# Attention and MLP in one kernel: from emission by budget to a hand-ordered pipeline of 32 head-pair steps

## Chip, core, metric

One core of a Trainium2 chip. The metric is device time in microseconds. Every time of a kernel is a median of several executions. Comparisons use runs in the fast state: a run counts as slow when it is over 1.5% above the fastest of the same kernel in its call. The kernel before itself spreads over 3%, so that in the call of e8, e9 and e11 seven of its eleven runs count as slow and in that of e12 six; the recorded medians of before in these calls include them, the ratios do not.

## The reference, cut to what matters

```python
# 8 batches, 8 heads, 576 queries, 16 beacon keys ahead of 576 keys, D = 64
scores = (q @ k_all.T) / sqrt(64); scores = where(causal, -1e9, scores)
a = exp(scores - max); a /= a.sum(-1)
x = (a @ v_all)                      # heads side by side: 4608 tokens x 512
h = x @ w_in                         # 512 -> 2048
out = (h * sigmoid(1.702 * h)) @ w_out   # 2048 -> 512
```

Beacon keys are seen by every query; the others are causal. Both kernels work in fp16 with fp32 sums, without subtracting the maximum, and use tanh for the sigmoid.

## The kernel before

It keeps scores transposed (keys on partitions) so that exp(scores) is at once an operand of AV. A pair of heads uses rows 0 to 63 and 64 to 127 of TensorE. The parts that the argument touches:

```python
# mask: a matmul of identity x tmask (-30000) into the scores' PSUM
nc.tensor.matmul(scA[0:kkw, 0:mw], ident[:, 0:kkw], tmask[:, mc0:mc0+mw], start=False, stop=True)
nc.scalar.activation(out=EjA[...], in_=scA[...], func=AFT.Exp, scale=0.125)   # one head, <= 512 columns
# AV: lhs = V and one column of ones, 65 columns; row 64 of the result is Z
nc.scalar.copy(out=zcb[r0:r0+1, 0:512], in_=oA[64:65, :])
# every four heads: 1/Z, then broadcast by a matmul with ones, then multiply on VectorE
nc.vector.reciprocal(out=rz[0:97, :], in_=zcb[0:97, :])           # 97 x 576
nc.tensor.matmul(pbc[0:64, :], ones128[r0:r0+1, :], rz[r0:r0+1, 0:512], ...)
nc.vector.tensor_tensor(out=xT[p][...], in0=pbc[0:64, :], in1=ox[...], op=ALU.mult)
# MLP1 tile: 4 matmuls of 384 columns, tanh on ScalarE, gate on VectorE (frees PSUM)
nc.scalar.activation(out=sig, in_=hps, func=AFT.Tanh, scale=0.851)
nc.vector.scalar_tensor_tensor(out=gt[...], in0=sig, scalar=1.0, in1=hps, op0=ALU.add, op1=ALU.mult)
# after each pair: up to 16 units of MLP in a row; where there is none, three warm-up matmuls
pump_mlp(MLP_BUDGET)
```

All PSUM comes from one pool of eight banks.

The softmax here doesn't subtract the row's maximum and nothing guards it: scores larger than these inputs give would overflow.

## Time and profile before

| | before |
|---|---|
| median of three runs | 540.97 us (535.39 to 541.63) |
| span of the profiled run | 536.4 us |
| mean granted TensorE clock | 0.916 |
| first MLP matmul | 68.6 us |
| two batches in the steady part (from one 64-matmul piece of the chain at 112.84 to the same piece at 239.00) | 126.16 us, so 63.1 a batch |

Part 1 of the page (busy time and share of each engine), the groups of three lines by form (line, engine, operation, shapes, count; busy us and mean ns; idle before), and the row of windows for the two batches (length, busy us of PE, PEld, DVE, ACT and POOL, clock, DMA share, GB/s), all of the kernel before:

```profile
PE 489.2 (91%) x3204; PEld 257.6 (48%) x3204; DVE 298.8 (56%) x553; ACT 271.5 (51%) x741; POOL 120.9 (23%) x164
```

```profile
L254 DVE RECIPROCAL rz<-zcb_cur 97x576 f16<-97x576 f32 x16 | 60.0, 3753 | 6.2 <-ACT zcb_cur L248 6.2
...
L187 PE MATMUL pu<-tmask,ident 128*128 128x128 f16 x96 | 23.2, 241 | 0.0
...
L201 ACT ACTIVATE EjA<-pu 128x512 f16<-128x512 f32 x32 | 19.1, 595 | 64.3 <-PE pu L194 39.0 <-PE pu L187 25.1
```

```profile
112.84:239.00 126.16, 120.62 (x800) 63.91 (x800) 74.34 (x139) 67.23 (x185) 27.33 (x35) 0.91 0.50 48
```

The shares alone say "TensorE, 91%". Three things qualify that. Busy time of a matmul is longer than the room it takes (an MLP2 matmul counts 389 ns in the groups by form, while one follows another every 216 ns), so overlapping matmuls hide idle slots. The clock of 0.91 in the steady part makes the same work longer. And one line of VectorE, the reciprocal, takes 3.75 us, five to eight times as long as the engine's other large groups (456 to 680 ns); everything behind it waits, as in the trace, where VectorE starts nothing else between 130.02 and 133.69 us.

### The profile page before, as it was taken

To read this page: it belongs to the slowest core of one execution; us is meant where nothing else is said; L and a number is where in the kernel's file an instruction comes from. 1 tells how busy PE (TensorE), PEld (TensorE's weight loads), DVE (VectorE), ACT (ScalarE), POOL (GpSimd) and SP (SyncE) were. 2 spreads that over 40 slices of the span, in tenths; PEclk is the share of its full clock that TensorE was granted. 3 is DMA by queue.
4 is the path that set the end of the run, shared out by engine and by line. 5 is a ranking of instruction groups with operands and counts; after the bars stand their busy time and mean duration, and the time that the engine had idled before them with its cause. 6 is when DMAs were issued, how large, how long until landed. Compare 5 with 4: busy or idle time off the path is not lost.

```text
span 536.4 us, 8324 instructions
## 1 busy us (share of the span) xinstructions
PE 489.2 (91%) x3204; PEld 257.6 (48%) x3204; DVE 298.8 (56%) x553; ACT 271.5 (51%) x741; POOL 120.9 (23%) x164
## 2 busy tenths in 40 slices
PE   1996998999999999999999999989989999949997
PEld 0453554555435455555445445545544545525543
DVE  1236587497624367677842436977851625878400
ACT  0472667467714269358631448577641446627411
POOL 9568850540004500270000900060000000000000
PEclk9997798599789999689969999899969999869999
DMA  9999990990016910190002960090001010000022
GB/s 94 175 173 142 93 89 2 66 70 1 2 39 74 160 40 2 12 122 3 2 0 79 125 88 21 2 89 2 1 0 72 29 59 21 1 1 2 20 79 78
DMA packets 122919, 28.59 MB, mean 53 GB/s; under 512 B 115712, under 2 KB 117760, under 8 KB 122880
## 3 DMA queue, kind: packets, MB, share of 16 engines
q0 software_dynamic: 117696, 18.62, 46.9%
q1 hardware_dynamic: 5184, 9.44, 4.6%
q8 instruction: 25, 0.41, 0.3%
q14 instruction: 14, 0.11, 0.1%
HBM read 37.22 MB, written 9.44 MB: 87 GB/s over the span
## 4 chain that ended last, share of the span: by engine, by line
PE 67%; ACT 11%; DVE 7%; POOL 5%; issue 5%; DMA 4%; ACTq 0%; DVEq 0%; POOLq 0%
PE pu L326 24%; PE pu L302 18%; PE pu L229 5%; PE pu L170 4%; ACT EjA L201 3%; PE pu L147 3%; DVE rz L254 3%; DMA w<-in_moe_w_in_dram 3%; PE pu L135 3%; PE pu L187 3%; ACT zcb_cur L247 3%; ACT EjB L207 2%; ACT sig L313 2%; DVE ox L244 2%; DVE g L314 2%
## 5 line engine op out<-in xcount | busy, mean ns | idle before, releaser
L302 PE MATMUL pu<-xT,w 128*128 128x384 f16 x768 | 131.3, 331 | 1.8 <-DVE g L314 1.1
L326 PE MATMUL pu<-w,g 128*128 128x512 f16 x576 | 130.8, 389 | 0.0
L313 ACT ACTIVATE sig<-pu 128x384 f16<-128x384 f32 x192 | 91.7, 491 | 51.7 <-PE pu L302 33.4
L201 ACT ACTIVATE EjA<-pu 128x512 f16<-128x512 f32 (+2 forms) x192 | 83.8, 442 | 64.9 <-PE pu L194 39.0
L314 DVE SCALAR_TENSOR_TENSOR g<-sig,pu 128x384 f16<-128x384 f16 x192 | 100.7, 549 | 26.5 <-ACT sig L313 17.4
L302 PEld LDWEIGHTS <-w 128*128 128x128 f16 x768 | 75.1, 99 | 55.1 <-issue 7.8
L244 DVE CAST ox<-pu 64x512 f16<-64x512 f32 x64 | 43.2, 675 | 101.6 <-PE pu L229 55.5
L326 PEld LDWEIGHTS <-g 128*128 128x128 f16 x576 | 56.7, 100 | 71.4 <-issue 8.3
L103 POOL DMA_DIRECT2D qb<-in_q_dram x40 | 34.5, 879 | 222.9 <-PE pu L135 218.4
L207 ACT ACTIVATE EjB<-pu 128x512 f16<-128x512 f32 (+2 forms) x192 | 83.0, 448 | 0.5 <-PE pu L194 0.2
L334 ACT ACTIVATE osb<-pu 128x512 f32<-128x512 f32 x36 | 21.5, 597 | 112.9 <-PE pu L326 94.7
L254 DVE RECIPROCAL rz<-zcb_cur 97x576 f16<-97x576 f32 x16 | 60.0, 3753 | 6.2 <-ACT zcb_cur L248 6.2
L177 PE MATMUL pu<-qTp,kTp 64*128 64x512 f16 (+2 forms) x192 | 56.9, 312 | 2.2 <-DVE g L314 1.4
L170 PE MATMUL pu<-qTp,kTp 64*128 64x512 f16 (+2 forms) x192 | 55.8, 313 | 3.4 <-ACT EjA L201 1.9
L247 ACT COPY zcb_cur<-pu 1x512 f32<-1x512 f32 x64 | 36.9, 577 | 31.0 <-DVE ox L244 30.0
L140 DVE COPY qTp<-pu 128x576 f16<-128x576 f16 x32 | 14.6, 456 | 56.3 <-PE pu L135 56.2
L283 DVE TENSOR_TENSOR xT<-pu,ox 64x512 f16<-64x512 f32 x64 | 43.5, 680 | 2.2 <-PE pu L261 0.7
L229 PEld LDWEIGHTS <-vb 128*65 128x65 f16 (+1 forms) x320 | 36.6, 129 | 9.1 <-issue 4.9
L236 PEld LDWEIGHTS <-vb 128*65 128x65 f16 (+1 forms) x320 | 35.5, 129 | 6.9 <-issue 1.9
L187 PE MATMUL pu<-tmask,ident 128*128 128x128 f16 (+2 forms) x160 | 38.4, 240 | 0.0
L194 PE MATMUL pu<-tmask,ident 128*128 128x128 f16 (+2 forms) x160 | 37.5, 234 | 0.0
L261 PE MATMUL pu<-rz,ones 1*64 1x512 f16 x64 | 17.5, 462 | 20.2 <-ACT zcb_cur L247 12.4
(42 smaller groups left out, 436.7 us busy)
## 6 DMA issues: line engine op xcount, KB each, us to landing
out_dram<-osb SPq DMA_DIRECT2D x36, 256.0 KB, 2.0
qb<-in_q_dram POOLq DMA_DIRECT2D x32, 128.0 KB, 4.4
kb<-in_k_dram POOLq DMA_DIRECT2D x32, 128.0 KB, 4.9
vb<-in_v_dram POOLq DMA_DIRECT2D x24, 128.0 KB, 4.4
w<-in_moe_w_in_dram POOLq DMA_DIRECT2D x4, 512.0 KB, 10.5
w<-in_moe_w_out_dram POOLq DMA_DIRECT2D x16, 128.0 KB, 4.9
vb<-in_v_dram POOLq DMA_DIRECT2D x8, 112.0 KB, 3.6
vb<-in_v_dram POOLq DMA_DIRECT2D x8, 80.0 KB, 4.8
```

The source lines that it names most:

```text
L170: nc.tensor.matmul(scA[0:kkw, 0:w], kTp[0:64, kk0 : kk0 + kkw], qTp[0:64, s0 + c : s0 + c + w], start=True, stop=not do_mask,)
L177: nc.tensor.matmul(scB[0:kkw, 0:w], kTp[64:128, kk0 : kk0 + kkw], qTp[64:128, s0 + c : s0 + c + w], start=True, stop=not do_mask,)
L187: nc.tensor.matmul(scA[0:kkw, 0:mw], ident[:, 0:kkw], tmask[:, mc0 : mc0 + mw], start=False, stop=True,)
L201: nc.scalar.activation(out=EjA[0:kkw, c : c + w], in_=scA[0:kkw, 0:w], func=AFT.Exp, scale=0.125,)
L207: nc.scalar.activation(out=EjB[0:kkw, c : c + w], in_=scB[0:kkw, 0:w], func=AFT.Exp, scale=0.125,)
L229: nc.tensor.matmul(oA[0 : D + 1, s0:512], lhs, ej[0:kkw, 0:wA], start=(j == 0), stop=(j == NJ - 1),)
L244: nc.vector.tensor_copy(out=ox[0:64, 0:512], in_=oA[0:64, :])
L254: nc.vector.reciprocal(out=rz[0:97, :], in_=zcb[0:97, :])
L302: nc.tensor.matmul(hps[:, :], w1t[kp][:, nt * P : (nt + 1) * P], xT[kp][:, tok0 : tok0 + MB], start=(kp == 0), stop=(kp == NKP - 1),)
L313: nc.scalar.activation(out=sig[:, :], in_=hps[:, :], func=AFT.Tanh, scale=0.851)
L314: nc.vector.scalar_tensor_tensor(out=gt[:, MB * blk : MB * blk + MB], in0=sig[:, :], scalar=1.0, in1=hps[:, :], op0=ALU.add, op1=ALU.mult,)
L326: nc.tensor.matmul(ops[:, :], gts[(r, nt)][:, mt * P : (mt + 1) * P], w2t[nt][:, :], start=(nt == 0), stop=(nt == NNT - 1),)
```

## The change

The intent: one step for each of the 32 pairs of heads, in which four score chunks of pair i, four AV halves of pair i-1 and transposes for the next batch are emitted with eight MLP slots between them (a slot is one MLP1 tile of 512 columns or a quarter of an MLP2 tile). The core of the 852-line diff, with cuts:

```diff
-                nc.tensor.matmul(scA[0:kkw, 0:mw], ident[:, 0:kkw], tmask[...], start=False, stop=True)
-                nc.scalar.activation(out=EjA[...], in_=scA[0:kkw, 0:w], func=AFT.Exp, scale=0.125)
+        nc.scalar.activation(out=E[:, :, choff[ci]:choff[ci]+o], in_=sc[:, :, 0:o], func=AFT.Exp, scale=0.125)  # both heads
+            if i < 8:   # mask on exp's output: min with 0 / 65504
+                    nc.vector.tensor_tensor(out=E[...], in0=E[...], in1=keep[...], op=ALU.min)
+            else:
+                nc.gpsimd.affine_select(out=blk, in_=blk, compare_op=ALU.is_ge, fill=0.0, ...)
...
-        lhs = vb[0:kkw, j, h, 0 : D + 1]
+        lhs = vb[0:kw, j, h, :]          # V beside 64 columns of ones: Z comes out on 64 rows
-        nc.vector.reciprocal(out=rz[0:97, :], in_=zcb[0:97, :])
-                nc.tensor.matmul(pbc[0:64, :], ones128[...], rz[...], ...)
+    z_gather(b, hf)   # DMA: Z of four heads to 64 partitions x 36 columns
+    z_recip(b, hf)    # next step: reciprocal of 36 columns, DMA to DRAM, DMA back, broadcast
+    norm(b, hf)       # the step after: 4 multiplications on GpSimd into xT
...
+    pss = ...(bufs=2)  # scores, two banks each
+    psu = ...(bufs=3)  # MLP1, AV, transposes
+    pso = ...(bufs=1)  # MLP2
...
+    for i in range(NSTEP + LAG):
+        run_later(i)                       # z_recip, norm, "batch ready"
+        ... att = 4 score chunks, 4 AV halves, [z_gather], transposes
+            if p == 0:
+                load_qk(nb, 0, H); load_bk(nb)      # next batch, GpSimd's queue, behind norm
+        for a in range(n):
+            att[a]()
+            want = (a + 1) * QUOTA // n
+            while done < want: mlp_slot(); done += 1
```

The mask matmuls, the broadcast matmuls, the warm-up matmuls, the copies of Z and the long reciprocal go. GpSimd gets masks and normalisation on top of issuing all input loads.

## The prediction

> **What bounds the kernel now.** I read the page first (busy tenths, granted clock, DMA row), then the chain of work that ended last in order of time, then the timeline of one pair of heads, then the table of windows.
>
> ```profile
> PE   1996998999999999999999999989989999949997
> ...
> PEclk9997798599789999689969999899969999869999
> DMA  9999990990016910190002960090001010000022
> ```
>
> TensorE is busy almost throughout, but its clock is not whole: the mean granted clock is 0.916. One window shows what a dip is:
>
> ```profile
> 142.20:152.40 10.20, 9.54 (x46) 4.46 (x47) 5.35 (x13) 4.08 (x15) 0.00 (x0) 0.50 0.01 2
> 500.00:520.00 20.00, 20.00 (x97) 9.29 (x95) 2.22 (x4) 4.50 (x9) 0.00 (x0) 1.00 0.14 53
> ```
>
> The clock (third figure from the end) is 0.50 in the first and 1.00 in the second. If it is always one or the other, (1 - 0.916)/0.5 = 17% of 536.4 us, some 90 us, ran at half clock, which costs up to 45 us. The chain tells what surrounds those stretches:
>
> ```profile
> 16.80 14.82 DMA w<-in_moe_w_in_dram
> ...
> 68.56 10.54 PE pu L302 x64
> ...
> 130.02 3.75 DVE rz L254
> 133.77 0.88 DVE g L314 x2
> ...
> 172.82 13.83 PE pu L326 x64
> ```
>
> (Columns: start, length, what.) Three readings. The first 68.6 us have no MLP: inputs and weights come in, and the POOL queue stands behind the w1 transfers. A dense MLP matmul of 512 columns takes 13.83/64 = 216 ns, one of 384 takes 10.54/64 = 165 ns (162 in the clean parts). And in between, a 3.75 us reciprocal over 97 rows holds VectorE while TensorE waits for the g that frees its PSUM. The two MLP groups are 768 x 162 ns + 576 x 216 ns = 249 us; so 536 - 249 - 68 = 219 us go to attention, softmax denominators, half clock and waits after the start. That is what the change can win.
>
> **What the Trainium skill says.** "TensorE: Matmul & The Clock Gate", Part 1, has a clock of half or whole rate only, whole after a busy window of about 3.4 us, half after an idle one. The windows above agree (0.50 and 1.00). "TensorEngine Tiling (Array Packing)", Key Properties: changing the tiling mode drains the engine, and separate tiles run in parallel. The timeline agrees with both:
>
> ```profile
> 123.32 0.39 PE L170 MATMUL pu<-qTp,kTp 64*128 64x512 f16 x1
> 123.32 0.39 PE L177 MATMUL pu<-qTp,kTp 64*128 64x512 f16 x1
> 123.64 0.22 PE L187 MATMUL pu<-tmask,ident 128*128 128x112 f16 x1
> ```
>
> Both heads' score matmuls (64 rows each) start together, so the pair costs one; the 128-row mask matmul starts 0.32 us later rather than 0.216, so a switch costs about 0.1 us (0.095 over many such pairs). "DMA: Bandwidth & Descriptors", SWDGE vs HWDGE vs iDMA: a casting transfer must come from GpSimd; here all loads of inputs and weights do, at 879 to 916 ns of POOL time each (part 5 of the page). "GPSIMD Engine Reference", 3.1: a two-input elementwise op takes about 2.6 cycles per element at 1.2 GHz. The kernel before has no such op, so the normalisation below is an estimate from that page.
>
> **The change, part by part, on TensorE at whole clock.**
> MLP: 144 tiles x 4 x 216 = 124.4 us, and 36 x 16 x 216 = 124.4 us: 248.8 us, the same columns as before.
> Scores: for a pair of heads 512+64+336+80+464+208 = 1664 columns, both heads together, 0.71 us; four chunks with two mode switches each, 8 x 0.095 = 0.76 us. So 1.47 us a pair, 47 us for 32. The mask matmuls go (40 groups of 128 columns and some, about 67 ns each: 320 x 67 = 21 us, plus half of the switches that they forced).
> AV: 1664 columns for each of two heads in 18 matmuls, 1.45 us a pair, 46 us. Before it was about 1.5, so no gain there.
> Transposes: q and k of a pair are 10 matmuls. Before, four of 128 columns take 66 ns each and the 64-row one with its switch 132: 0.40 us for five. So 0.79 us a pair plus 0.44 us a batch for the beacon: about 26 us, and some 7 more for the first batch's 96-column form.
> The 1/Z broadcast (L261, L270: 128 matmuls, some 18 us), the 36 warm matmuls (8 us) and the reciprocal of 3.75 us x 16 go. Z now comes out of AV on 64 rows and takes a way through DRAM with reciprocals of 36 columns (about 0.3 us), three steps ahead of its use.
> Sum for TensorE: 249 + 47 + 46 + 33 = 375 us. It stays the bound.
>
> The others, by rows of before. ScalarE: exp of four chunks of 1024, 960, 928 and 416 columns; a 512-column activation takes 595 ns, back to back a stretch of N columns costs about 0.83N + 60 ns, so 3.0 us a step and 96 us in all (167 us busy before in twice-as-many small ones); tanh 144 x 0.6 = 86, output 36 x 0.6 = 21, q copies 32 x 0.67 = 21: about 225 to 240 us. VectorE: gate 144 x 0.68 = 98 (549 ns for 384 columns, plus 128/0.96), AV copies 128 x 0.44 = 56, k copies 15, masks of the first eight steps about 13: 190 us. POOL: 148 issues x 0.88 = 130, masks 120 x 0.4 = 48, normalisation 64 x 1.4 = 90: 268 us. All below TensorE.
>
> **The time, stage by stage.** The start. Step 0 can begin at about 6 us. But step 1 already transposes batch 1, whose q and k are issued behind w1 on the same queue. Before, by 50 us four tensors' worth had landed (batch 0, w1, w2, batch 1's q and k: 14.3 MB read, 300 GB/s); after, q and k of batch 1 come after batch 0 and w1, 10 MB, about 34 us; w2, V of batch 1 and q, k of batch 2 then come one after another until about 58 us, where step 5 wants them. So step 7, the first with MLP slots (batch 0 is marked ready there), begins at about 64 to 66 us. That is no earlier than before, with one more pair done.
> From there TensorE has 249 of MLP, 25 x 1.47 of scores, 26 x 1.45 of AV and 19 of transposes: 342 us.
> PSUM waits. MLP1, AV and transposes share three banks (before: eight for all). An MLP1 tile holds its bank for 0.65 + 0.39 (the last matmul's end) + 0.60 tanh + 0.68 gate = 2.35 us. With AV halves in between, the fourth claim comes after 2.1 us; the wait is some 0.28 us a slot, about 1.2 us in a step with eight MLP1 tiles; there are 14 of those: 17 us. MLP2 has one bank: 0.17 + 0.05 + 0.6 us until it is emptied, against 0.36 us of other work, so 0.45 us at most of 36: with the last ones about 12 us.
> Masks and normalisation on POOL behind eleven issues (10 us) in the first step of a batch: 1 us a batch, 8 us. Tail: output scaling 0.6 and store 2 us, 3.5 us.
> Sum: 66 + 342 + 17 + 12 + 8 + 3.5 = 448.5; measured medians lie some us above the profiled span (541 against 536): 451 us.
>
> **The rivals.** (a) Three PSUM banks are too few and ScalarE or VectorE become the pace. For: a step of eight MLP1 tiles has 3.0 + 4.8 us of ScalarE and 7.7 us of VectorE in some 11 us, each in strict order, so a tile's 2.35 us can grow to 3.3. Against: before, 64 MLP1 matmuls ran at 165 ns with the same chain of tanh and gate. Each further 0.5 us a tile costs 14 x 8 x 0.5 = 56 us at worst: 480 to 500. (b) POOL becomes the bound. For: 34 us of its work in a batch of about 47, in order, with issues ahead of masks that AV needs, and a two-input op on 64 partitions that no trace here prices. If it takes twice my estimate, POOL is at 45 of 47 us: 470 to 490. (c) Nothing waits: slots cover the waits, the start shortens because the first batch's q and k move in longer pieces and MLP starts at 55 us: 375 + 35 = 410 us. (d) The transfers eat the gain: the start stays on DMA until 80 us, as the issues of batch 1 wait behind w1: 465.
>
> **Range and chances.** Floor 375 plus an empty start is about 400; I see no way under 410. (a), (b) and (d) together would make 500. Eight in ten: 418 to 488. For a result within 2% of 541, some 80 us of new waits would have to arise beyond those counted: 3%; slower: 2%.
>
> **What would show each step.** Start: the first L302-like matmul at about 65 us, after a wait for a DMA of batch 1 or 2. Clock: mean at 0.94 or more and 1.00 after 70 us; if it dips there, the windows have idle stretches that I don't foresee. MLP matmuls at 216 ns of dense running. PSUM: TensorE's waits in the mlp1 lines put down to VectorE's gate at 0.2 to 0.5 us, some 20 us in all, and waits of MLP2 for ScalarE's scaling about 12 us. Rows: exp of 1024 columns near 1.04 us, normalisation near 1.4 us, POOL near half busy. Wrong would be: waits of AV for POOL masks over 15 us, of MLP1 for POOL's normalisation, or TensorE's own sum over 400 us at whole clock.

## The result

| | before | after |
|---|---|---|
| median | 538.18 us (4 runs) | 476.66 us (475.82 to 480.68, 4 runs) |
| profiled span | 536.4 us | 474.5 us |
| mean granted clock | 0.916 | 0.941 |
| first MLP matmul | 68.6 us | 89.8 us |
| from there to the end | 467.8 us | 384.7 us |
| a steady batch | 63.1 us | 48.2 us |

The ratio is 0.8879 (95% interval 0.8807 to 0.8951). A ratio is the mean time of one kernel's fast runs over that of the other's in the same rounds, so it is not quite the ratio of the medians quoted. The gain of 62 us has two parts of opposite sign: the part after the first MLP matmul became 83 us shorter, the start 21 us longer.

The kernel after, part 1 and rows of part 2 of its page (40 slices of 11.9 us):

```profile
PE 396.0 (83%) x2584; PEld 201.8 (43%) x2584; DVE 193.0 (41%) x410; ACT 222.8 (47%) x341; POOL 251.3 (53%) x348
...
PE   2505555889999999899989998999899999899985
...
PEclk9955675899999999999999999999999999999999
DMA  9999939959614981399129911990203112100111
```

Nearly all half-clock time is now in the first eight slices. (1 - 0.941)/0.5 x 474.5 is 56 us, as estimated for before, where it was 90 us all along the run. The row of windows for one steady batch and three groups of part 5:

```profile
190.64:238.84 48.20, 44.54 (x293) 21.91 (x292) 19.92 (x39) 25.95 (x41) 32.23 (x47) 1.00 0.80 85
```

```profile
L392 DVE SCALAR_TENSOR_TENSOR g<-sig,u 128x512 f16<-128x512 f16 x144 | 99.0, 687 | 104.9 <-ACT sig L391 104.8
L354 POOL TENSOR_TENSOR xT<-O,rz 64x576 f16<-64x576 f32 x64 | 89.6, 1400 | 79.9 <-DMA rz<-zd 76.3
...
L274 POOL TENSOR_SCALAR_AFFINE_SELECT E<-E 128x256 f16<-128x256 f16 (+2 forms) x120 | 43.1, 395 | 67.0 <-ACT E L252 66.3
```

The clock is 1.00 throughout the batch. VectorE has 20 us of work in 48, GpSimd 32. The view of waits (engine, line, what was waited for: us in total, times, longest), from the first MLP matmul to the end, has just these for TensorE:

```profile
PE u L382 <- DVE g L392: 12.4, 20, 0.7
PE o L408 <- ACT osb L417: 9.7, 25, 0.7
PE s L244 <- ACT E L252: 2.3, 5, 0.5
```

L382 is MLP1 and waits for the gate to free one of three banks; L408 is MLP2 and waits for its single bank; L244 is a score chunk and waits for exp. Together they come to 24.4 us, under 1 us each.

Where did the start go? The chain of work that ended last, of the kernel after, in order of time (start, length, what):

```profile
18.18 11.96 DMA w<-in_moe_w_in_dram
...
33.54 4.91 DMA bk<-in_beacon_k_dram
...
48.54 5.64 DMA zc<-O
...
57.16 4.40 DMA rz<-zd
61.70 1.40 POOL xT L354
...
67.83 4.25 POOL qn L114 x5
72.08 2.88 POOL kn L114 x4
...
76.20 3.43 DMA bk<-in_beacon_k_dram
```

Batch 1's beacon arrives at 38.4 us because its issue stood behind w1. Then Z of the first two pairs goes to DRAM and back, GpSimd normalises (61.7 to 67.5 us), and only behind that it issues batch 2's q, k and beacon, which arrive at 79.6 us. The transposes of batch 2 stand in TensorE's order before the first MLP slot.

So the first theory, "Q": GpSimd's strict order makes loads wait for Z. Its rival, "D": the DMA engines are full in the start, and the order is of no matter.

### The profile page after: what moved, and what is told of

It reads as the page before. It is cut to its first block, busy times and chain, and to the rows that moved or that the text cites. A ratio compares the mean times of both kernels' runs of the same rounds, so it can differ in the third digit from the quotient of the medians.

```text
span 474.5 us, 6853 instructions
## 1 busy us (share of the span) xinstructions
PE 396.0 (83%) x2584; PEld 201.8 (43%) x2584; DVE 193.0 (41%) x410; ACT 222.8 (47%) x341; POOL 251.3 (53%) x348
## 4 chain that ended last, share of the span: by engine, by line
PE 59%; ACT 17%; POOL 7%; DMA 7%; DVE 5%; issue 4%; ACTq 0%; POOLq 0%; DVEq 0%
PE o L408 26%; PE u L382 19%; ACT E L252 8%; PE u L310 6%; ACT sig L391 5%; PE u L189 4%; DVE g L392 4%; PE s L244 3%; ACT osb L417 3%; DMA w<-in_moe_w_in_dram 3%; DMA bk<-in_beacon_k_dram 2%; POOL kn L114 1%; POOL vb L136 1%; DMA zc<-O 1%; POOL xT L354 1%
## 5 line engine op out<-in xcount | busy, mean ns | idle before, releaser
L382 PE MATMUL u<-xT,w 128*128 128x512 f16 (+1 forms) x640 | 144.7, 358 | 12.5 <-DVE g L392 12.4
L408 PE MATMUL o<-w,g 128*128 128x512 f16 x576 | 144.1, 379 | 9.7 <-ACT osb L417 9.7
L392 DVE SCALAR_TENSOR_TENSOR g<-sig,u 128x512 f16<-128x512 f16 x144 | 99.0, 687 | 104.9 <-ACT sig L391 104.8
L354 POOL TENSOR_TENSOR xT<-O,rz 64x576 f16<-64x576 f32 x64 | 89.6, 1400 | 79.9 <-DMA rz<-zd 76.3
L391 ACT ACTIVATE sig<-u 128x512 f16<-128x512 f32 x144 | 87.6, 609 | 77.3 <-PE u L382 72.9
L252 ACT ACTIVATE E<-s 128x1024 f16<-128x1024 f32 (+3 forms) x128 | 104.7, 876 | 14.8 <-PE s L244 8.8
L317 DVE COPY O<-u 128x288 f32<-128x288 f32 x128 | 56.3, 453 | 71.2 <-PE u L310 69.9
L382 PEld LDWEIGHTS <-w 128*128 128x128 f16 x640 | 56.8, 97 | 63.3 <-issue 20.4
L408 PEld LDWEIGHTS <-g 128*128 128x128 f16 x576 | 50.2, 97 | 63.1 <-issue 15.6
L310 PE MATMUL u<-E,vb 128*128 128x288 f16 (+6 forms) x576 | 69.5, 260 | 5.3 <-DVE O L317 5.1
L310 PEld LDWEIGHTS <-vb 128*128 128x128 f16 (+1 forms) x576 | 52.5, 104 | 36.8 <-issue 12.2
L244 PE MATMUL s<-qT,kT 64*128 64x80 f16 (+5 forms) x384 | 44.1, 307 | 18.4 <-ACT E L252 9.9
L244 PEld LDWEIGHTS <-kT 64*128 64x128 f16 x384 | 17.1, 99 | 58.6 <-issue 46.2
L267 DVE TENSOR_TENSOR E<-E,keep 128x128 f16<-128x128 f16 (+2 forms) x80 | 17.1, 271 | 14.0 <-ACT E L252 13.6
```

Of the source, the lines that this page charges most:

```text
L244: nc.tensor.matmul(sc[:, x, o : o + e - a], kT[r : r + 64, p, j * P : (j + 1) * P], qT[r : r + 64, p, a:e], start=True, stop=True,)
L252: nc.scalar.activation(out=E[:, :, choff[ci] : choff[ci] + o], in_=sc[:, :, 0:o], func=AFT.Exp, scale=0.125,)
L310: nc.tensor.matmul(u[:, lo - qa : hi - qa], lhs, E[0:kw, x, col : col + hi - lo], start=(n == 0), stop=(n == len(mm) - 1),)
L317: nc.vector.tensor_copy(out=O[:, p % 2, qa:qe], in_=u[:, :])
L354: nc.gpsimd.tensor_tensor(out=xT[r : r + 64, p, c : c + S], in0=O[r : r + 64, a, :], in1=rz[r : r + 64, a, :], op=ALU.mult,)
L382: nc.tensor.matmul(u[:, o : o + w], w1t[:, kp, nt * P : (nt + 1) * P], xT[:, kp, m : m + w], start=(kp == 0), stop=(kp == NKP - 1),)
```

## The experiments

### The order of loads, three single changes

**e1_loads_first**: from batch 2 on, loads ahead of the normalisation.

```diff
+        if 0 < b < B - 1 and p == 0:
+            issue_qk(b + 1)
         run_later(i)
```

> Only the order on GpSimd's queue changes: from batch 2 on, the q, k and beacon loads of the next batch are issued ahead of the normalisation instead of behind it. In the changed kernel the first MLP matmul starts at 89.8 us, and the chain before it is AV of pair 1, the trip of Z through DRAM, four normalisations, eleven issues, the beacon of batch 2 at 79.6 us. Theory Q (GpSimd's strict order makes the loads wait for Z): the wait for batch 2's beacon goes, MLP starts at 80 to 84 us, the whole takes 467 to 471 us. Rival D (the 16 DMA engines are full in the start, order does not matter): MLP starts within 2 us of 89.8, 475 to 477 us.

Measured: 476.21 us, first MLP matmul at 89.3 us. The wait for batch 2's beacon is gone, and yet nothing was won. The timeline of e1 shows another holder:

```profile
67.32 5.92 POOL L354 TENSOR_TENSOR xT<-O,rz 64x576 f16<-64x576 f32 x4
...
71.01 3.21 DVE L267 TENSOR_TENSOR E<-E,keep 128x112 f16<-128x112 f16 x10
...
78.01 5.91 POOL L354 TENSOR_TENSOR xT<-O,rz 64x576 f16<-64x576 f32 x4
...
79.81 4.46 DVE L267 TENSOR_TENSOR E<-E,keep 128x128 f16<-128x128 f16 x8 [0.20 <-ACT E L252]
```

L267 is the mask on VectorE, a minimum of two SBUF operands. Beside GpSimd's multiplications eight of them take 4.46 us. In e5 below, where GpSimd multiplies nothing at that time, ten take 1.30:

```profile
65.18 1.30 DVE L267 TENSOR_TENSOR E<-E,keep 128x112 f16<-128x112 f16 x10
```

That agrees with the Trainium skill, "SBUF — State Buffer", Who interferes with whom: a VectorE instruction with two SBUF inputs contends with a GpSimd instruction that reads SBUF.

**e2_b1_first**: batch 1 ahead of w1.

```diff
+    new_nat(1); new_qk(1); load_qk(1, 0, H); load_bk(1)
     load_w1(0)
```

> Only the order again: batch 1's q, k and beacon are issued ahead of w1, not behind it. Theory Q: the wait for batch 1's beacon that ends at 38.4 us ends at about 24 us, all that follows up to the normalisation moves by 12 to 14 us, and as batch 2's loads still stand behind it, MLP starts at 76 to 79 us: 462 to 466 us. Rival D: the same bytes have to come before MLP can start, so it starts at 88 to 90 us and the time is 474 to 477 us.

Measured: 475.13 us, first MLP matmul at 89.3 us. Step 2 starts at 31.5 us instead of 42.1, but batch 2's beacon still arrives only at 76.0 us, 3.6 us earlier, and the masks then take 5 us beside the normalisation.

**e3_w2_late**: w2 issued behind V of batch 2 (step 5).

```diff
-                if b == 0:
-                    for c in range(4): load_w2(c)
...
+                if b == 1:
+                    for c in range(4): load_w2(c)
```

> The 4.2 MB of w2 leave the start and are issued behind the V loads of batch 2 (step 5); all other orders stay. Rival D (bandwidth): the start is shorter by the 10 us which w2 takes, MLP at about 80 us, 466 us. Theory Q: batch 2's loads stand behind the normalisation as before; only Z's trip, whose gather took 5.6 us among w2's transfers, gets 2 to 4 us shorter: MLP at 84 to 88 us, 471 to 475 us.

Measured: 476.66 us, first MLP matmul at 88.9 us. e3 was made to catch D, but D's 466 us did not come, and Q's 471 to 475 us did not either. w2 was issued at 77.7 us instead of 34.5. With its 4.2 MB out of the way the trip of the first Z took 8.6 us (1.74 + 2.40 + 4.44) instead of 12.5, as Q had said, and batch 2's beacon arrived at 76.0 us, 3.6 us earlier. But most of that was lost again before the first MLP step: the last four masks on VectorE took 2.96 us beside GpSimd's next multiplications. So volume alone is not the cause. The numbers of e1 and e2 look like rival D's; the three runs together say that the start has several chains of nearly one length.

### Both orders at once, and the trip of Z

**e4_order**: batch 1 (with V) ahead of w1; q and k of batch b+2 at the end of step p = 3 of batch b, so ahead of the normalisation; w2 behind batch 2.

```diff
+        if p == 3 and b + 2 < B:
+            new_nat(b + 2); load_qk(b + 2, 0, H); load_bk(b + 2)
+            if b == 0:
+                for c in range(4): load_w2(c)
```

> Both orders at once, as a candidate for a better kernel: batch 1 ahead of w1, every later batch's q and k at the end of the step three ahead of its transposes, so ahead of the normalisation, w2 behind batch 2. Theory Q: no wait for a beacon after 25 us, MLP starts at 58 to 66 us, the rest as in the changed kernel (385 us): 445 to 453 us. Rival D: bytes needed before MLP are nearly the same, start at 80 us or later, 466 us or more.

Measured: 465.71 us, first MLP matmul at 75.5 us: 11 us better than the changed kernel, and none of the three changes alone gave more than 1.5. The start shrank by 14 us rather than by the 24 or more of Q, so neither theory's range was met. What its chain of work shows from 56.7 us to the first full MLP tile is the trip of Z and three multiplications behind it, and that trip is slow:

```profile
56.66 4.70 DMA zc<-O
...
61.85 4.62 DMA zd<-rc
...
67.07 8.32 DMA rz<-zd
```

Those 17.6 us overlap transfers of w2 and V of batch 2; e11 below tests whether these are what slows it.

**e5_trip**: e4_order, with V of batch 2 and w2 emitted at the end of step 6, and batch 0's normalisation on VectorE.

```diff
+                eng = nc.vector if b == 0 else nc.gpsimd
+                eng.tensor_tensor(out=xT[...], in0=O[...], in1=rz[...], op=ALU.mult)
...
+        if i == 6:
+            load_v(2, j, 0, H) for all j; load_w2(c) for all c
```

> On top of the order of e4_order: w2 and the V loads of batch 2 are issued only at the end of step 6, and batch 0's normalisation runs on VectorE instead of GpSimd. In e4_order the first MLP tiles still wait for batch 0's second normalisation, whose Z trip took 4.7 + 4.6 + 8.3 us among the loads (2.1 + 2.5 + 4.4 in the steady part). Theory T (the trip of Z shares the DMA engines with bulk loads and is the last chain of the start): MLP starts at 66 to 70 us and runs on without the 2.6 us wait for a normalisation; 452 to 457 us. Rival S (the steps themselves, at half clock and with masks on VectorE, set the start): MLP not before 74 us, 463 to 466 us.

Measured: 475.06 us, first MLP matmul at 88.1 us (one of four runs took 593.09 us and is left out). The experiment failed in an instructive way. With the normalisation gone from GpSimd, nothing held its queue back, so w2 was issued at 65.8 us, in the middle of the trip again: "later in the program" was not later in time. And VectorE now stood waiting for Z itself, 7.2 us before the first multiplication of the second Z, with masks and AV copies behind it.

### What slots and masks are worth in the changed kernel

**e6_slots_end**: all eight slots after the attention pieces.

```diff
-            want = (a + 1) * QUOTA // n
+            want = (a + 1) // n * QUOTA
```

> The changed kernel with one thing undone: the eight MLP slots of a step come after all attention pieces instead of between them. Theory P (the slots cover the waits of attention for exp): scores of a step take 1.5 us on TensorE, their four exps 3.3 us on ScalarE, so TensorE waits about 1.8 us a step; rows of MLP1 tiles lose their 1.3 us of PSUM waits in every second step, MLP2 gets 0.5 us more. Net +1 to +1.5 us in each of 25 steps: 500 to 515 us. Rival: the same total of waits moves elsewhere, 470 to 485 us.

Measured: 504.92 us, the median of three fast runs (498.55 to 505.00). The slots between the pieces are worth 22 to 28 us, as theory P says; that the time goes into waits for exp was not read from a trace, since the profile fell into the slow run described at the end.

**e7_no_mask**: no mask on the output of exp. Its output is wrong, which doesn't matter for the time.

```diff
-        for (j, a, e) in CH[ci]:
-            ... min on VectorE or affine_select on GpSimd
```

> Wrong result on purpose: no mask at all, neither on VectorE nor on GpSimd. Theory H (masks are hidden in the steady part): the steady batch stays at 48.2 us; only in the start, where VectorE's masks stood between GpSimd's normalisations and took 2.2 to 5 us for eight or ten of them, MLP starts 2 to 5 us earlier: 471 to 475 us. Rival: AV waits for masks in each step, 0.5 us or more for 25 steps: 462 us or less.

Measured: 478.57 us against 476.66 for the changed kernel; a steady batch takes 48.2 us as before. The masks are hidden in the steady part. The second half of the theory failed: the start did not shorten (first MLP matmul at 92.1 us in the profiled run), though the masks' collision with the normalisation is real. The page of e7 shows where, and that the run does not test the collision: the start still waited for batch 2's beacon, which took 7.70 us to land instead of 3.43 and so arrived at 82.6 us. Why it took longer is open.

```profile
74.89 7.70 DMA bk<-in_beacon_k_dram
```

### What the parts are worth in the kernel before

**e8_before_no_mask**: the mask matmuls left out. Its output is wrong, which doesn't matter for the time.

```diff
-                do_mask = c == 0
+                do_mask = False
```

> The kernel before with one part alone, wrong on purpose: the mask matmuls are left out, nothing is put in their place. By the sums of the prediction they are 320 matmuls of 67 ns, 21 us, and they force eight of ten mode switches of a pair, 0.76 us x 32 = 24 us. Theory M (TensorE's own sum sets the pace of before in the attention stretches): 45 us go, 490 to 500 us. Rival A (there TensorE waits for ScalarE's exps and for PSUM anyway, so the waits fill the room): 5 to 20 us go, 515 to 533 us.

Measured: 531.40 us, ratio 1.0039 (0.9972 to 1.0107): nothing. Before itself ran between 526.84 and 543.45 us, its four fast runs up to 533.11. One thing did change: the granted clock was 0.908 to 0.914 in the four runs without masks and 0.929 to 0.945 in before's fast ones. By the estimate above that is some 94 us at half clock against 68, so part of the work saved may have been lost to the clock.

**e9_before_recip**: a reciprocal of 36 columns instead of 576. Its output is wrong, which doesn't matter for the time.

```diff
-            nc.vector.reciprocal(out=rz[0:97, :], in_=zcb[0:97, :])
+            nc.vector.reciprocal(out=rz[0:97, 0:36], in_=zcb[0:97, 0:36])
+        nc.gpsimd.memset(rz[0:97, 36:S], 0.003)
```

> The kernel before with one part alone, wrong on purpose: the reciprocal works on 36 of 576 columns (3.4 us less of VectorE, 16 times), the other columns of 1/Z are filled with a constant by GpSimd. Theory V (the reciprocal stands in front of the gates of MLP1 that free PSUM, TensorE stops behind it and its clock falls to half): 16 x 1 to 2 us of wait go, 505 to 522 us, and the mean granted clock rises by 0.02 or more. Rival: other work covers it, less than 5 us, 532 to 540 us.

Measured: 499.07 us, ratio 0.9420 (0.9349 to 0.9490): some 31 us less than before's fast runs, more than theory V had. Part 1 and the clock row of its page:

```profile
PE 462.0 (93%) x3204; PEld 247.7 (50%) x3204; DVE 244.9 (49%) x553; ACT 272.1 (55%) x741; POOL 129.5 (26%) x180
...
PEclk9998599999999999789999999999999999989999
```

TensorE issues the same 3204 matmuls and is busy 27 us less than in the profile of before, whose span is 38.5 us longer, and most dips of the clock are gone: mean 0.969. At half clock are (1 - 0.969)/0.5 x 497.9 = 31 us, an estimate as before, and 27 to 31 in e9's four runs, against 58 to 75 in before's four fast runs. The means differ by 39 us; if TensorE worked through these, the clock accounts for up to 20 of the 31 us. One dip in the timeline of before, with the reciprocal at 130.02 to 133.77 us and half clock from 142.15 to 152.39:

```profile
134.24 4.89 PE L302 MATMUL pu<-xT,w 128*128 128x384 f16 x28 [0.35 <-DVE g L314]
...
140.40 0.19 PE L177 MATMUL pu<-qTp,kTp 64*128 64x64 f16 x1 [0.46 <-DVE g L314]
```

The stops behind the late gates are short (0.35 and 0.46 us here); the 10.2 us at half clock that follow can cost up to 5. That the long reciprocal brings the loss is shown by e9; how the 31 us divide between stops and clock is an estimate.

**e12_both**: e8 and e9 together. Its output is wrong, which doesn't matter for the time.

> The kernel before, wrong on purpose, with the two cuts of e8 and e9 at once: no mask matmuls and a reciprocal of 36 columns. Alone the first gave nothing (531 us against 536, ratio 1.00), the second 6% (499 us). Theory B (the masks' 45 us of TensorE were hidden behind the stops at the reciprocal): with these gone they count, 455 to 480 us. Rival C (in before's attention stretches TensorE waits for exp and PSUM, reciprocal or not): 488 to 500 us, and TensorE's busy share falls below the 93% of e9.

Measured: 502.22 us, ratio 0.9461 (0.9386 to 0.9535), no better than e9 alone. Part 1 and the clock row of its page:

```profile
PE 433.7 (87%) x2884; PEld 237.9 (48%) x2884; DVE 244.9 (49%) x553; ACT 270.7 (54%) x741; POOL 129.4 (26%) x180
...
PEclk9996599999999999898999999899899999889999
```

TensorE lost 28 us of busy time and the kernel lost none: the share fell from 93 to 87%. In the order of before, the mask matmuls filled room in which TensorE would have waited. Rival C holds, with a median 2 us above its range; theory B's 455 to 480 us are out. The clock fell here too, to 0.942 to 0.959 in six runs against 0.969 to 0.973 in e9's, so some of the room went into half clock; how much was not separated.

### Order within a step, and the best version

**e10_mixed**: score chunk, AV half, score chunk, AV half, instead of four and four.

```diff
+        if 1 <= i < NSTEP:
+            att[0:8] = [att[k // 2 + 4 * (k % 2)] for k in range(8)]
```

> The changed kernel with score chunks and AV halves taken in turn (score, AV, score, AV ...) instead of four scores and then four AV halves; same work. Theory W (TensorE's waits of some 5 us a batch come from three shared PSUM banks filled in the AV part while ScalarE still works off the exps): between an MLP1 tile and the claim that needs its bank there are then 2.4 us, about its hold of 2.4, so the waits of 0.67 us twice in a step with MLP1 tiles go to 0.2 or less: 1 us less in each of 14 steps, 462 to 468 us. Rival (ScalarE's order: tanh now stands behind an exp everywhere): 474 to 482 us.

Measured: 471.55 us; a steady batch takes 47.4 us. That is about 5 us better, half of what theory W had and between the two ranges. The steps with MLP1 tiles became 1.0 and 1.6 us shorter (p = 0 and p = 3), but that with p = 1 longer by 1.6 us: 13.3 instead of 11.7. A likely reason is that AV now comes sooner behind the masks of p = 0, which stand behind GpSimd's ten issues: the view of waits of e10 has 6.8 us in eight waits of AV for these masks, and the changed kernel's has none.

**e11_best**: all of that: e10, the order of e4, loads of a batch spread over its steps, and V of batch 2 and w2 behind batch 0's second normalisation on GpSimd, which holds them back in time as well.

```diff
+            if i == 6:                      # after norm(0, 1) in GpSimd's queue
+                load_v(2, j, 0, H) for all j; load_w2(c) for all c
...
+        if b >= 2: a few of next batch's V, q and k loads at the end of each step
```

> A candidate that joins what the runs showed: score and AV pieces in turn, batch 1 ahead of w1, q and k of later batches long ahead of their use and spread over steps, and V of batch 2 and w2 issued behind batch 0's second normalisation on GpSimd, so that its Z trip meets no bulk loads. In e4_order that trip (17.6 us where the steady one takes 9) and the normalisation behind it ended at 80 us; MLP should start at 68 to 73 us and the first MLP step take 12 to 13 us instead of 17.8. The masks of a batch's first step no longer stand behind ten issues, which cost e10_mixed 1.6 us a batch. Theory: 446 to 455 us. Rival (the start is held by the steps themselves at half clock): MLP at 75 us or later, 458 to 463 us.

Measured: 453.17 us (452.36 to 454.84, six runs), ratio to before 0.8562 (0.8516 to 0.8608), correct. It beats both kernels: some 77 us under before's fast runs (526.84 to 533.11), and 23 us under the changed kernel's median. The first MLP matmul is at 72.0 us, and the p = 1 step is back at 11.7. The trip of the second Z of batch 0, with no bulk loads beside it, takes 7.5 us instead of e4's 17.6:

```profile
53.77 2.21 DMA zc<-O
...
56.47 1.70 DMA zd<-rc
...
58.25 3.63 DMA rz<-zd
```

What each part of e11 gives was not run apart. One loss is left, in its chain of work:

```profile
74.74 15.43 DMA w<-in_moe_w_out_dram
```

GpSimd's next issues wait there for w2 to land, the masks stand behind them, and in step 9, the first with MLP2, one AV matmul waits 5.58 us for a mask; the step takes 20.4 us instead of 11.7. An earlier w2 should win some 8 us more; that was not run.

## Why the prediction was right, and where it was off

**The total.** 451 us was predicted, 477 measured, inside 418 to 488. The direction and the size of the gain held.

**After the first MLP matmul** the sum gave 342 + 17 + 12 + 8 + 3.5 = 382.5 us; 384.7 were measured. The costs of single operations came out near: multiplications on GpSimd 1.40 us as estimated, the gate 0.687 instead of 0.68, busy GpSimd 251 instead of 268 us. (Two sums slip: VectorE's four parts make 182, not 190, with 193 measured, and an MLP1 tile's hold makes 2.32, not 2.35 us.) That the sum itself is so near is partly luck, since two errors of it cancel. Waits were 24.4 us instead of 37: for the gate 12.4 instead of 17, for MLP2's bank 9.7 instead of 12, for masks behind GpSimd's issues none instead of 8, and 2.3 of scores for exp that had been left out. With the tail of about 4 us that leaves some 356 us for TensorE's own work and short gaps, 14 more than counted. TensorE stayed the bound and its clock stayed whole from slice nine on. The two windows of the prediction do show the two clock rates, but not the times that it cites for the change between them: the 10.2 us at 0.50 had TensorE 94% busy by the profile, and in the 3.4 us before them it was busy 2.49 us, so no idle window of that length went ahead.

**The start was the mis-sized term.** The step "so step 7 ... begins at about 64 to 66 us" failed: it was 89.8 us, and these 24 us are nearly all of the error. The working counted bytes behind bytes (batch 2's q and k by 58 us). It overlooked that their issue stands in GpSimd's queue behind a normalisation that waits for a trip of 12.5 us (5.64 + 2.46 + 4.40) through DRAM, though the diff shows that order. It also took the early steps to keep pace with the loads; between 23 and 88 us TensorE was busy 31 of 65 us at a mean clock of 0.58. e1, e2 and e3 then showed that no single chain is the cause: loads behind the normalisation, masks against the normalisation, and Z's trip among bulk loads end within a few microseconds of one another. Only moving several (e4, e11) shortened it, to 75.5 and 72.0 us.

**Rivals.** (d) named the right place and over half of the size, "the start stays on DMA until 80 us", but put it down to transfers; e3 speaks against volume alone. (a) fell: the waits were smaller than counted. (b) fell in the steady part: GpSimd is busy 32 of 48 us there, and without masks the batch is no shorter (e7). (c) fell with the start.

**Where the gain came from** the prediction left in one sum. The runs weigh the parts: in the kernel before, the long reciprocal alone held some 31 us (e9), the 21 us of mask matmuls with their switches nothing (e8, e12); in the changed kernel, the interleaving of slots holds 22 to 28 us (e6). The prediction listed the mask matmuls as 21 us that go, which is true for TensorE's sum and was not true for the time. The parts do not simply add up, and the broadcast and warm-up matmuls were not tried alone.

## What to carry to other kernels

Before counting what removed matmuls save, ask whether TensorE would merely have waited in their place; one long instruction on the engine that frees PSUM can cost more than hundreds of matmuls (here 31 us against nothing), probably in good part through the clock. When an engine both issues loads and computes, write down its queue in order: a load stands behind everything emitted before it, also behind an operation that waits for a round trip through DRAM. When a change at one of several equally long chains wins nothing, that does not acquit the chain; move two at once before you drop the theory.

## What the Trainium skill lacked or had wrong

- "TensorE: Matmul & The Clock Gate", Part 1, notes that the clock records can be unreliable and that the clock was seen stuck low for over 50 us. One execution of e6_slots_end was slow as a whole, 1001 us, and its trace holds no clock record at all (its page has no clock row; the 1.00 listed for it is not a measurement): in its chain of work 16 matmuls of 512 columns took 9.70 us, 606 ns each instead of 216. The page has no whole execution of that kind. No conclusion here rests on it.

```profile
303.01 9.70 PE o L408 x16
```

- "VectorE: DVE Perf Modes" says how a reciprocal is computed, by a divide repeated eight times, but gives no time. Here 576 fp32 columns take 3753 ns and 36 take 364 ns (after) or 378 (e9), some 6.3 ns a column; a cast of 512 columns takes 675 ns.
- "DMA: Bandwidth & Descriptors" has a fixed cost of about 2 us a transfer, fitted to transfers issued from GpSimd. A chain of three small dependent ones issued from SyncE takes 5.64 + 2.46 + 4.40 us in the start of the changed kernel, 4.70 + 4.62 + 8.32 us in e4 among the loads of w2 and V, and 2.21 + 1.70 + 3.63 us in e11 without them. The page says that transfers interleave on the same 16 engines, but gives no time that a small one loses among bulk ones.
- "TensorEngine Tiling (Array Packing)", Key Properties, says that a change of tiling mode drains the engine, without a price; about 0.1 us here, between the 64-row scores and the 128-row mask in the timeline of before.
